# 256-byte allocation of the DMA tiles in a fused lightning-attention and mixture-of-depths kernel

## The chip, the cores and the metric

The kernel runs on one core of a Trainium2 chip. The metric is device time in microseconds (us) of one execution, the median of several runs. The core has the engines PE (TensorE; PEld is its weight load), DVE (VectorE), ACT (ScalarE) and POOL (GpSimd), SP (SyncE), which here only issues DMAs, and 16 DMA engines that move data between the chip's main memory (DRAM) and SBUF, the on-chip memory of 128 partitions.

## The reference

Four batches of eight heads with 768 positions of 64 elements, all float32. Attention runs in blocks of 64 positions with a decaying state, and its output is then taken as rows of 512 elements, of which the 128 best of each batch go through a two-layer expert:

```
for b in range(nb):                       # blocks of 64 positions, all batches and heads
    intra = (qb @ kb.T * Dmask) @ vb
    inter = (qb * lam_pow) @ kv_state
    out[:, :, sl] = intra + inter
    kv_state = lam_block * kv_state + (kb * rev_pow).T @ vb
x = out.transpose(0, 2, 1, 3).reshape(B, S, H * D)      # 4 x 768 x 512
scores = x @ w_gate
for b in range(B):
    top = the 128 rows of x[b] with the highest scores
    h = relu(x[b, top] @ w1); ye = h @ w2               # 512 x 1024 and 1024 x 512
    out[b, top] = x[b, top] + sigmoid(scores[b, top]) * ye
```

## The kernel before

The work is cut into 24 groups g, six per batch, of 128 positions of all eight heads. For every group `load` (L74) issues three DMAs on SP, `kn`, `qn` and `vn`, each 128 partitions by 8 heads by 64 elements: 256 KB in 1,024 pieces of 256 bytes, since one head's row of one position is 256 contiguous bytes in DRAM. The tiles lie in pool `ld` with six buffers per name, and a group's load is issued four to six groups ahead of its use (`loads_to`, `ahead`). On the same SP queue, in an order written out in the tables `WEIGHTS_WITH` and `STORES_WITH`, stand the 16 loads of the expert's weights (`w1_sb`, `w2_sb`, 128 rows of 2 KB each, L101 and L106) and the 24 stores of `x_b` (`store`, L380, 128 rows of 2 KB), so a store that waits for its data holds up the loads behind it.

In a group, PE transposes `kn` and `qn` (L207), forms the scores (L234 in the first nine, wide groups, L241 later), the state products from `kd` and `vn` (L274, L283), and the outputs (L326, L338, L346). POOL makes `kd`, the decayed keys (L191), the decayed queries `qs` (L219, L221) and the decayed state (L296). ACT copies the transposes and the output rows `x_b` (L368 to L376) out of PSUM. DVE masks the scores (L251, L257), adds the state (L315), makes the gate scores from `x_b` and `wg_b` (L388), and ranks rows (L418). In the wide groups PE transposes the gate scores (L408) right behind L388.

When a batch is ranked, POOL gathers its 128 rows from the output in DRAM (`fetch`, L483, tile `xs`), PE runs the expert (L496, L533, L545, the last batch in halves at L570), and DVE makes `y` or `y_half`, which POOL scatters back (L562, L586). Pieces of an earlier batch's expert are set between the steps of later groups by the table `PIECES`. Tiles are placed by the pools one behind the other, at multiples of 32 bytes.

Of the kernel before, what the change touches and what calls it, by code (L numbers as in the profile page):

```python
# [8 lines left out]
FP32 = mybir.dt.float32  # L9
# [8 lines left out]
def kernel(  # L18
# [14 lines left out]
    B, H, S, D = q.shape  # L33
    HD = H * D
    F = moe_w1.shape[1]
# [3 lines left out]
    NT = S // L  # L39
    NHP = H // 2  # L40
    NDC = HD // 128
    NFC = F // 128
# [3 lines left out]
    assert 0 <= CAP < S  # L46

    AHEAD = 6
    WIDE = 9
    WEIGHTS_WITH = {  # L50
        "kn": {11: 1, 12: 2, 13: 1, 14: 1, 15: 1, 16: 1},
# [11 lines left out]
    const = ctx.enter_context(tc.tile_pool(name="const", bufs=1))  # L63
    ld = ctx.enter_context(tc.tile_pool(name="ld", bufs=AHEAD))
    att = ctx.enter_context(tc.tile_pool(name="att", bufs=3))
    xpool = ctx.enter_context(tc.tile_pool(name="xpool", bufs=2))
    mod = ctx.enter_context(tc.tile_pool(name="mod", bufs=2))
# [6 lines left out]
    def load(g):  # L74
        b, c = divmod(g, NT)
        rows = slice(c * L, (c + 1) * L)
        tiles = []
        for name, src in (("kn", k), ("qn", q), ("vn", v)):
            t = ld.tile([128, H, D], FP32, name=name)
            nc.sync.dma_start(out=t[:], in_=src[b, :, rows, :].rearrange("h p d -> p h d"))  # L80
            tiles.append(t)
            for _ in range(WEIGHTS_WITH[name].get(g, 0)):
                weights.pop(0)()
            for s in STORES_WITH[name].get(g, ()):
                store(s)
        loaded[g] = tiles
# [4 lines left out]
    nc.scalar.dma_start(out=wg_row[:], in_=moe_w_gate.unsqueeze(0))  # L91
    for g in range(3):
        load(g)
    wg_b = const.tile([128, HD], FP32, name="wg_b")
    w1_sb = const.tile([128, NDC, F], FP32, name="w1_sb")
    w2_sb = const.tile([128, NFC, HD], FP32, name="w2_sb")

    def w1_load(f0, n, c):
        def do():
# [76 lines left out]
    x_bs, scs = {}, {}  # L176
# [6 lines left out]
    def wide(g):  # L183
        return g < WIDE

# [175 lines left out]
    def outputs(g):  # L361
        b, t = divmod(g, NT)
        if t == 0:
            x_bs[b] = xpool.tile([128, NT, NHP, 2, D], FP32, name="x_b")
            scs[b] = xpool.tile([128, NT], FP32, name="sc")
        x_b = x_bs[b]
        if wide(g):
            nc.scalar.copy(  # L368
                out=x_b[:, t].rearrange("p b a e -> p a b e"),
                in_=o_[:, :, : NHP * D].rearrange("p a (b e) -> p a b e", e=D),  # L370
            )
            return
        po = [o_[:, hh, : NHP * D].rearrange("p (b e) -> p b e", e=D) for hh in range(2)]
        nc.scalar.copy(out=x_b[:, t, :, 0, :], in_=po[0])
        for c in range(2):
            nc.scalar.copy(out=x_b[half[c], t, :, 1, :], in_=po[1][half[1 - c]])  # L376

    def store(g):
        b, t = divmod(g, NT)
        nc.sync.dma_start(  # L380
            out=out[b, t * L : (t + 1) * L, :],
            in_=x_bs[b][:, t].rearrange("p a b e -> p (a b e)"),
        )
# [9 lines left out]
    def rows_upto(b):  # L393
        return out[0 : b + 1].flatten_outer_dims()
# [83 lines left out]
    def rows_at(b, i):  # L478
        return bass.IndirectOffsetOnAxis(ap=toks[b, i][:, 0:1], axis=0)

    def fetch(b, i):
        xs = mod.tile([128, HD], FP32, name="xs")
        nc.gpsimd.indirect_dma_start(  # L483
            out=xs[:], out_offset=None, in_=rows_upto(b), in_offset=rows_at(b, i),
        )
        xss[b, i] = xs

    def expert(b, i, last=False):
# [51 lines left out]
        def back(f):  # L540
            def do():
                if f == 0:
                    keep["py"] = bank(hold=True)
                py = keep["py"]
                nc.tensor.matmul(  # L545
                    py[:], lhsT=keep["hs"][:, f, :], rhs=w2_sb[:, f, :],
                    start=(f == 0), stop=(f == NFC - 1),
                )
                if f + 1 == NFC:
                    after.append(finish)  # L550
            return do

        def finish():
            py = keep["py"]
            held.clear()
            free[:] = [x for x in free if x is not py] + [py]
            y = mod.tile([128, HD], FP32, name="y")
            nc.vector.scalar_tensor_tensor(
                out=y[:], in0=py[:], scalar=keep["g"][:], in1=xss[b, i][:],
                op0=ALU.mult, op1=ALU.add,  # L560
            )
            nc.gpsimd.indirect_dma_start(  # L562
                out=rows_upto(b), out_offset=rows_at(b, i), in_=y[:], in_offset=None,
            )

        def half_back(f, c):
            def do():
                if f == 0:
                    keep["py"] = bank()
                nc.tensor.matmul(  # L570
                    keep["py"][:, : HD // 2], lhsT=keep["hs"][:, f, :],
                    rhs=w2_sb[:, f, c * (HD // 2) : (c + 1) * (HD // 2)],
                    start=(f == 0), stop=(f == NFC - 1),
                )
                if f + 1 == NFC:
                    half_finish(c)
            return do

        def half_finish(c):
            cs = slice(c * (HD // 2), (c + 1) * (HD // 2))  # L580
            y = mod.tile([128, HD // 2], FP32, name="y_half")
            nc.vector.scalar_tensor_tensor(
                out=y[:], in0=keep["py"][:, : HD // 2], scalar=keep["g"][:],
                in1=xss[b, i][:, cs], op0=ALU.mult, op1=ALU.add,
            )
            nc.gpsimd.indirect_dma_start(  # L586
                out=rows_upto(b).rearrange("r (c e) -> (r c) e", c=2),
                out_offset=bass.IndirectOffsetOnAxis(ap=keep["at"][:, c : c + 1], axis=0),
                in_=y[:], in_offset=None,
            )  # L590
# [54 lines left out]
    def products(n):  # L645
        for _ in range(min(n, len(pieces))):
            pieces.pop(0)()

    def ahead(g):
        return min(4 + max(0, (g - 12) // 2), AHEAD)  # L650

# [4 lines left out]
    def loads_to(n):  # L656
        while next_load[0] < min(n, NG):
            load(next_load[0])
            next_load[0] += 1
# [12 lines left out]
    def get(b):  # L672
        for i in range(NGR):
            fetch(b, i)

    for g in range(-1, NG):
# [16 lines left out]
        if wide(g):  # L693
# [5 lines left out]
            if g >= 0:  # L699
                next_state(2 * g + 2)  # L700
                from_scores(g)
                outputs(g)
                if g not in kept:
                    store(g)
            else:
                state_products(0)
                next_state(0)
# [38 lines left out]
        now = PIECES.get(g, (1, 1, 1))  # L746
        if g == WIDE:
            products(1)
# [19 lines left out]
        products(now[1])  # L768
        from_scores(g)
        outputs(g)  # L770
        if g not in kept:
            store(g)
# [77 lines left out]
```

## Time and profile before

| what | value |
|---|---|
| median of 3 runs | 177.38 us (176.01 to 177.85) |
| the profiled execution | 176.31 us, of which the span from the first to the last instruction is 174.5 us |
| PE busy | 161.6 us (93%), granted clock at its upper level through the span |
| other engines busy | DVE 101.7, POOL 92.7, ACT 71.9 us |
| bytes moved by DMA | 31.96 MB in 81,475 packets |

Busy time of PE is modelled from pipelined matmuls, so a busy PE is not PE at its peak, and idle time of an engine off the path costs nothing. What counts for a change to DMA is which idle time a DMA ended. A packet is what a DMA engine moves as one unit: here 256 bytes for `kn`, `qn`, `vn`, 2 KB for weights and stores.

### The profile page before, as it was taken

The page shows a single profiled execution, that of the slowest core. Times are in us where ns is not written, and L with a number is a line of the kernel's source. Part 1 is how long each engine was busy: PE and PEld are TensorE (multiplying, and loading weights), DVE is VectorE, ACT ScalarE, POOL GpSimd, SP SyncE. Part 2 cuts the span into 40 slices and gives each one's busy share as a digit, 9 for nine tenths or more (in the row PEclk, how much of TensorE's full clock was granted, in tenths as well). Part 3 has the DMA queues.
Part 4 walks back from the last instruction along what each step waited for, and adds up shares of the span by engine and source line. Part 5 has one row for each costly group of instructions (what it writes and reads, how often), then busy time and mean ns, then how long its engine had stood idle before and what let it go on. Part 6 is the DMA issues. An engine that isn't in the chain of part 4 may idle for free.

```text
span 174.5 us, 7862 instructions
## 1 busy us (share of the span) xinstructions
PE 161.6 (93%) x3440; PEld 133.1 (76%) x3440; DVE 101.7 (58%) x227; ACT 71.9 (41%) x192; POOL 92.7 (53%) x101
## 2 busy tenths in 40 slices
PE   6898999999998999998999999999899899989990
PEld 6767888788786989765768999866669698459970
DVE  2566966777946834756547994675477856340011
ACT  2244365553344635543535544633555354013100
POOL 2249975818796554466595856455777700220022
PEclk9999999999999999999999999999999999999999
DMA  4999899999989999998999897998931111011000
GB/s 91 219 219 193 193 227 244 236 280 274 243 202 266 261 260 274 269 282 198 240 263 215 210 208 170 270 309 202 227 147 64 64 64 60 0 60 64 0 30 30
DMA packets 81475, 31.96 MB, mean 183 GB/s; under 512 B 75809, under 2 KB 75809, under 8 KB 81442
## 3 DMA queue, kind: packets, MB, share of 16 engines
q1 hardware_dynamic: 80640, 29.37, 71.0%
q0 software_dynamic: 656, 2.10, 4.0%
q8 instruction: 27, 0.44, 1.1%
q14 instruction: 6, 0.05, 0.1%
q10 hardware_dynamic: 146, 0.01, 0.0%
HBM read 24.12 MB, written 7.34 MB: 180 GB/s over the span
## 4 chain that ended last, share of the span: by engine, by line
PE 67%; DMA 12%; issue 6%; POOL 5%; DVE 4%; ACT 2%; SPq 2%; POOLq 1%; DVEq 0%
PE m L533 15%; PE m L207 9%; PE m L545 9%; DMA w_sb<-in_moe_w_dram 6%; PE o L338 5%; PE o L326 4%; PE o L346 4%; PE su L283 4%; DMA vn<-in_v_dram 3%; PE su L241 3%; PE m L274 3%; DVE xg L388 2%; PE m L137 2%; PE su L234 2%; PE m L570 2%
## 5 line engine op out<-in xcount | busy, mean ns | idle before, releaser
L418 DVE SCALAR_TENSOR_TENSOR table<-sc_row,sc,lead 128x128 bf16<-128x128 f32 (+5 forms) x24 | 28.1, 1170 | 14.6 <-ACT sc_row L411 14.0
L533 PE MATMUL m<-xsT,w_sb 128*128 128x128 f32 x256 | 34.1, 282 | 0.7 <-ACT xsT L503 0.5
L533 PEld LDWEIGHTS m<-xsT,w_sb 128*128 128x128 f32 x256 | 30.6, 192 | 1.7 <-ACT xsT L503 0.7
L221 POOL TENSOR_TENSOR qs<-qT,qpow 128x512 f32<-128x512 f32 x15 | 21.0, 1400 | 13.5 <-ACT qT L211 12.0
L388 DVE CUSTOM_DVE_ANT_0 xg<-x_b,wg_b 128x512 f32<-128x512 f32 x24 | 21.7, 903 | 8.7 <-ACT x_b L368 8.1
L545 PE MATMUL m<-w_sb,hs 128*128 128x512 f32 x48 | 24.9, 621 | 0.4 <-DMA w_sb<-in_moe_w_dram 0.4
L296 POOL TENSOR_TENSOR decayed<-state,decay 128x256 f32<-128x256 f32 x25 | 18.6, 745 | 12.4 <-DVE state L315 11.7
L537 ACT ACTIVATE hs<-m 128x128 f32<-128x128 f32 x32 | 8.9, 278 | 25.6 <-PE m L533 24.0
L315 DVE TENSOR_TENSOR state<-su,decayed 128x256 f32<-128x256 f32 x25 | 10.5, 421 | 14.3 <-PE su L283 9.2
L211 ACT COPY qT<-m 128x512 f32<-128x512 f32 x24 | 14.1, 586 | 9.8 <-PE m L207 6.7
L191 POOL TENSOR_TENSOR kd<-kn,kpow 128x512 f32<-128x512 f32 x15 | 16.2, 1082 | 0.5 <-DMA kn<-in_k_dram 0.5
L211 ACT COPY kT<-m 128x512 f32<-128x512 f32 x24 | 14.2, 592 | 3.6 <-PE m L207 3.6
L326 PE MATMUL o<-state,qs 64*64 64x64 f32 x672 | 15.3, 224 | 0.0
L207 PE MATMUL m<-ident,qn 128*128 128x128 f32 x96 | 15.1, 281 | 0.0
L207 PE MATMUL m<-ident,kn 128*128 128x128 f32 x96 | 14.9, 279 | 0.0
L411 ACT COPY sc_row<-m 128x128 f32<-128x128 f32 x24 | 6.3, 264 | 20.4 <-PE m L408 17.8
L326 PEld LDWEIGHTS o<-state,qs 64*64 64x64 f32 x672 | 12.4, 134 | 2.7 <-issue 2.3
L219 POOL TENSOR_TENSOR qs<-qT,qpow 128x512 f32<-128x512 f32 x7 | 9.8, 1404 | 6.9 <-ACT qT L211 6.9
L191 POOL TENSOR_TENSOR kd<-kn,kpow_w 128x512 f32<-128x512 f32 x9 | 9.9, 1100 | 6.0 <-DVE kpow_w L148 5.2
L207 PEld LDWEIGHTS m<-ident,qn 128*128 128x128 f32 x96 | 11.4, 144 | 2.0 <-issue 1.1
L283 PE MATMUL su<-vn,kd 64*64 64x64 f32 x432 | 10.4, 221 | 2.4 <-DMA vn<-in_v_dram 1.1
L346 PEld LDWEIGHTS o<-vn,p 64*64 64x64 f32 x480 | 8.4, 134 | 5.0 <-ACT sc_row L411 2.3
(85 smaller groups left out, 256.2 us busy)
## 6 DMA issues: line engine op xcount, KB each, us to landing
kn<-in_k_dram SPq DMA_DIRECT2D x24, 256.0 KB, 5.4
qn<-in_q_dram SPq DMA_DIRECT2D x24, 256.0 KB, 5.3
vn<-in_v_dram SPq DMA_DIRECT2D x24, 256.0 KB, 5.6
out_dram<-x_b SPq DMA_DIRECT2D x24, 256.0 KB, 4.6
w_sb<-in_moe_w_dram SPq DMA_DIRECT2D x16, 256.0 KB, 5.4
xs<-out_dram,tok POOLq DMA_INDIRECT x4, 4.5
out_dram<-y,tok POOLq DMA_INDIRECT x3, 3.4
out_dram<-y_half,half_at POOLq DMA_INDIRECT x2, 2.4
```

Source lines behind the costliest of these rows:

```text
L191: nc.gpsimd.tensor_tensor(out=kd[:], in0=loaded[g][0][:], in1=pw[:].rearrange("p a b -> p (a b)").unsqueeze(2).broadcast_to([128, H, D]), ...
L207: nc.tensor.transpose(tp[:, hp * L : (hp + 1) * L], in_=t[:, 2 * hp : 2 * hp + 2, :], identity=ident[:])
L211: nc.scalar.copy(out=dst[:].rearrange("p a i -> p (a i)"), in_=tp[:])
L221: nc.gpsimd.tensor_tensor(out=qs[:].rearrange("p a (c i) -> p a c i", c=2), in0=qTs[g].rearrange("p a (c i) -> p a c i", c=2), in1=qpow[:, ...
L283: nc.tensor.matmul(su[half[hh], c, NHP * C + hp * D : NHP * C + (hp + 1) * D], lhsT=kd[half[c], h, :], rhs=vn[half[c], h, :], start=True, ...
L296: nc.gpsimd.tensor_tensor(out=t[:], in0=states[n][:], in1=(decay_w if wide(g) else decay)[:], op=ALU.mult)
L326: nc.tensor.matmul(o_[half[c if wide(g) else hh ^ c], hh, hp * D : (hp + 1) * D], lhsT=qs[half[hh], hp, half[c]], rhs=states[n][half[hh], ...
L346: nc.tensor.matmul(o_[half[hh ^ c], hh, hp * D : (hp + 1) * D], lhsT=p[half[c], hh, hp * C : (hp + 1) * C], rhs=vn[half[c], 2 * hp + hh, : ...
L388: nc.vector.tensor_tensor_reduce(out=xg[:], in0=x_bs[b][:, t].rearrange("p a b e -> p (a b e)"), in1=wg_b[:], scale=1.0, scalar=0.0, op0=A ...
L418: nc.vector.scalar_tensor_tensor(out=table[:, : (t + 1) * L], in0=rows_[b][:, : (t + 1) * L], scalar=scs[b][:, t : t + 1], in1=lead[:, (NT ...
L533: nc.tensor.matmul(ph, lhsT=w1_sb[:, dc, f * 128 : (f + 1) * 128], rhs=keep["xsT"][:, dc, :], start=(dc == 0), stop=(dc == NDC - 1),)
L545: nc.tensor.matmul(py[:], lhsT=keep["hs"][:, f, :], rhs=w2_sb[:, f, :], start=(f == 0), stop=(f == NFC - 1),)
```

## The change

Tiles of ten names are allocated at a multiple of 256 bytes on each partition: nine that a DMA writes or reads, and the gate vector `wg_b`, which ACT writes. No instruction is added, removed or moved on any engine: the lists of the five engines are the same but for source line numbers, which rise by one behind the new constant.

```diff
+    LINE = 256
...
-            t = ld.tile([128, H, D], FP32, name=name)
+            t = ld.tile([128, H, D], FP32, name=name, align_bytes=LINE)
...
-    wg_b = const.tile([128, HD], FP32, name="wg_b")
-    w1_sb = const.tile([128, NDC, F], FP32, name="w1_sb")
-    w2_sb = const.tile([128, NFC, HD], FP32, name="w2_sb")
+    wg_b = const.tile([128, HD], FP32, name="wg_b", align_bytes=LINE)
+    w1_sb = const.tile([128, NDC, F], FP32, name="w1_sb", align_bytes=LINE)
+    w2_sb = const.tile([128, NFC, HD], FP32, name="w2_sb", align_bytes=LINE)
...
-            x_bs[b] = xpool.tile([128, NT, NHP, 2, D], FP32, name="x_b")
+            x_bs[b] = xpool.tile([128, NT, NHP, 2, D], FP32, name="x_b", align_bytes=LINE)
...
-        xs = mod.tile([128, HD], FP32, name="xs")
+        xs = mod.tile([128, HD], FP32, name="xs", align_bytes=LINE)
...
-            y = mod.tile([128, HD], FP32, name="y")
+            y = mod.tile([128, HD], FP32, name="y", align_bytes=LINE)
...
-            y = mod.tile([128, HD // 2], FP32, name="y_half")
+            y = mod.tile([128, HD // 2], FP32, name="y_half", align_bytes=LINE)
```

The built programs give every tile's byte address on its partition. All buffers of one name have the same distance past a multiple of 256:

| tile | first buffer before | past a multiple of 256 | first buffer after | past a multiple of 256 |
|---|---|---|---|---|
| `kn` | 74,976 | 224 | 75,776 | 0 |
| `qn` | 87,264 | 224 | 88,320 | 0 |
| `vn` | 99,552 | 224 | 100,864 | 0 |
| `wg_b` | 18,592 | 160 | 18,688 | 0 |
| `w1_sb` | 20,640 | 160 | 20,992 | 0 |
| `w2_sb` | 37,024 | 160 | 37,632 | 0 |
| `x_b` | 150,752 | 224 | 152,320 | 0 |
| `xs` | 191,904 | 160 | 193,536 | 0 |
| `y` | 208,416 | 32 | 210,432 | 0 |
| `y_half` | 212,576 | 96 | 214,784 | 0 |

The tiles behind them move along: `kd`, for one, from 224 to 32 past a multiple of 256. `lam_b`, whose rows are 32 bytes, stays at 128 past. The highest byte used grows from 214,624 to 216,832.

## Rows read from the trace of the kernel before

**Rows 1.** The page: engines' busy time, and the 40 slices of the span.

```profile
PE 161.6 (93%) x3440; PEld 133.1 (76%) x3440; DVE 101.7 (58%) x227; ACT 71.9 (41%) x192; POOL 92.7 (53%) x101
...
PE   6898999999998999998999999999899899989990
...
PEclk9999999999999999999999999999999999999999
DMA  4999899999989999998999897998931111011000
GB/s 91 219 219 193 193 227 244 236 280 274 243 202 266 261 260 274 269 282 198 240 263 215 210 208 170 270 309 202 227 147 64 64 64 60 0 60 64 0 30 30
```

**Rows 2.** PE's waits: who was waited for, us in total, times, longest.

```profile
PE m L408 <- DVE sc L388: 1.3, 4, 0.6
PE su L283 <- DMA vn<-in_v_dram: 1.1, 3, 0.5
...
PE su L283 <- POOL kd L191: 0.4, 1, 0.4
PE m L496 <- DMA xs<-out_dram,tok: 0.4, 1, 0.4
PE m L545 <- DMA w_sb<-in_moe_w_dram: 0.4, 1, 0.4
...
PE m L533 <- DMA w_sb<-in_moe_w_dram: 0.3, 1, 0.3
```

**Rows 3.** POOL's waits for the keys: us in total, times, longest.

```profile
POOL kd L191 <- DMA kn<-in_k_dram: 1.3, 3, 0.8
```

**Rows 4.** DMA view, 5 to 15 us: packets; then queue, packets, MB, share.

```profile
DMA packets 8628, 2.18 MB, mean 218 GB/s; under 512 B 8628, under 2 KB 8628, under 8 KB 8628
...
q1 hardware_dynamic: 8628, 2.18, 130.5%
```

**Rows 5.** SP's queue in order of time: start, us it took, what.

```profile
9.44 1.10 SPq L80 DMA_DIRECT2D vn<-in_v_dram  x1
...
63.78 0.38 SPq L80 DMA_DIRECT2D kn<-in_k_dram  x1
```

**Rows 6.** The DMA view, 121.8 to 122.8 us, the last loads.

```profile
DMA packets 1116, 0.29 MB, mean 285 GB/s; under 512 B 1114, under 2 KB 1114, under 8 KB 1116
...
q1 hardware_dynamic: 1116, 0.29, 125.5%
```

**Rows 7.** The DMA view, 90 to 105 us, loads alone on q1.

```profile
q1 hardware_dynamic: 10470, 2.64, 82.4%
```

**Rows 8.** SP's waits, the longest: who was waited for, us, times, longest.

```profile
SPq L380 <- ACT x_b L376: 11.4, 3, 6.0
...
SPq L80 <- POOL decayed L296: 4.0, 3, 3.0
SPq L80 <- POOL kd L191: 3.2, 5, 0.9
```

**Rows 9.** The DMA view, 2 to 5 us: lam_b, in rows of 32 bytes.

```profile
q10 hardware_dynamic: 127, 0.01, 2.2%
```

**Rows 10.** The DMA view, 130 to 150 us: stores of x_b.

```profile
q1 hardware_dynamic: 576, 1.05, 14.1%
```

**Rows 11.** The DMA view, 133.7 to 135 us: a scatter of y.

```profile
q0 software_dynamic: 79, 0.26, 54.1%
```

**Rows 12.** Single lines' instructions: duration ns min/median/max, first and last start us.

```profile
L388 DVE CUSTOM_DVE_ANT_0 xg<-x_b,wg_b x24: 678/842/1564, 14.4 to 145.5; 128x512 f32<-128x512 f32 x24
...
L515 DVE CUSTOM_DVE_ANT_0 xg<-xs,wg_b x4: 676/680/1746, 60.5 to 156.2; 128x512 f32<-128x512 f32 x4
...
L207 PE MATMUL m<-ident,qn x96: 272/273/421, 6.4 to 135.5; 128*128 128x128 f32 x96
...
L496 PE MATMUL m<-ident,xs x16: 272/273/327, 53.2 to 155.0; 128*128 128x128 f32 x16
```

**Rows 13.** The page: q1, packets, MB, share of 16 engines over the span.

```profile
q1 hardware_dynamic: 80640, 29.37, 71.0%
```

## The prediction

> **What bounds the kernel now.** First the page: PE is busy 161.6 of 174.5 us, at the upper clock level throughout, and the slices show it full from the first to the last but a few us, while the DMA row is also near full for the first 28 slices, some 122 us [rows 1]. Both are candidates, and the change touches only DMA, so the question is how much of PE's idle time a DMA ended. PE's list of waits answers it: three waits for `vn` cost 1.1 us, one each for `xs`, a `w_sb` of the first layer and one of the second 0.4, 0.4 and 0.3, together 2.2 us; one for `kd`, which stands behind a gather, 0.4 [rows 2]. So all that a faster stream of transfers can give directly is 2.2 to 2.6 us of 176. POOL's three waits for `kn` add 1.3 us of its own idle time [rows 3], of which PE feels a part at most in the start.
>
> Then I asked how near its limit the stream is. From 5 to 15 us, with loads alone queued, 8,628 packets take 130.5% of 16 engines [rows 4]: 1.305 x 160 / 8,628 = 24.2 ns each, overlapping, and one starts on each engine every 160 / 8,628 = 18.5 ns. That is a full stream at 218 GB/s: SP needs 1.10 us to issue one 256 KB load here, against 0.38 us for one where the queue has room [rows 5]. Later it is not full: the last loads run at 285 GB/s, 1.255 x 16 / 1,116 = 18.0 ns a packet and one start per engine every 14.3 ns [rows 6], and from 90 to 105 us q1 has packets for 82.4% of the time only [rows 7]. What holds SP there is its own order: stores wait 11.4 us for `x_b`, loads 4.0 and 3.2 us for buffers that POOL still reads [rows 8]. A faster engine does not shorten those.
>
> **The change part by part.** No instruction moves and no wait is added; ten names change their address.
>
> *Packets of the loads.* 24 groups x 3 loads x 1,024 = 73,728 packets of 256 bytes were written 224 past a multiple of 256, so each crosses one such boundary (32 bytes before it, 224 behind); after, none does. The trace has no load into an aligned tile, so the cost of the crossing is bounded. One end: nothing (a loss has no row: `lam_b` and all loads read DRAM as before, and crossing less is no more work). The other, for a packet that is not held up: the 127 packets on the queue of `lam_b`, nearly all 32 bytes at 128 past, cross nothing and take 0.022 x 48 us / 127 = 8.3 ns [rows 9]. A 2 KB store packet: 0.141 x 320 = 45.1 us, less some 0.5 us for 64 small completions, over 512 packets, 87.1 ns [rows 10]. From 256 bytes to 2 KB that is (87.1 - 18.0) / 1,792 = 0.0386 ns a byte, so a packet of 256 bytes that costs what the 32-byte one costs plus its 224 bytes more would take 8.3 + 8.6 = 16.9 ns: 1.1 ns under 18.0, or 6%. For a packet in the full stretch the far end is the spacing of the late loads, 14.3 instead of 18.5 ns, if the crossings are what fills the stretch; but the late loads cross the same boundary and run at 285 GB/s, so a crossing alone does not cost 18.5 ns. I take nothing, the value of the straight line through 256 bytes and 2 KB: it meets zero bytes at 18.0 - 256 x 0.0386 = 8.1 ns, close to the 7.1 that the 32-byte packet leaves when its own 32 bytes are taken off, so hardly anything is left for a crossing.
>
> *Stores, gathers and scatters.* `x_b` was read from 224 past, `y` from 32 past. The scatter of `y` has 64 packets of two rows (4 KB): 0.541 x 1.3 x 16 = 11.25 us, less 0.1 for 15 small ones, over 64 is 174 ns, or 87.0 per row of 2 KB, against 87.1 for a row of `x_b` [rows 10, 11]. Two very different offsets, one price: the offset costs nothing that these rows can show. If a row lost all that separates it from 2,048 x 0.0386 = 79 ns, 8 ns of 87 (9%), 24 stores of 128 rows would give 24 x 128 x 8 / 16 = 1.5 us of the stream, beside loads, on no path of PE but through the fetch behind a store. The last scatter, `y_half`, is the tail: 32 packets on 16 engines, two each, some 0.02 us at that price. I take nothing.
>
> The Trainium skill, "DMA: Bandwidth & Descriptors", section "How a descriptor splits into AXI transactions", speaks for the change: a transaction starts at a multiple of 256 bytes, and what lies between that and a descriptor's start is fetched for nothing, in beats of 32 bytes. By it a row of `x_b` would need 71 beats and one of `y` 65, 8% apart; the two rows above are equal, so this trace does not bear it out for reads of SBUF, and whether writes into SBUF follow it no run here shows. By its beats a load's packet would fall from 15 to 8; the rival below does without them.
>
> *Compute on the moved tiles.* DVE's gate product reads `x_b` at 224 past in 678 ns at least, the expert's reads `xs` at 160 past in 676; PE's transposes of `qn` at 224 and `xs` at 160 are both 273 ns [rows 12]. Engines do not feel the offset, so `kd` at 32 instead of 224 and the other moved tiles cost nothing.
>
> *Sum.* Against the profiled execution: 176.31 - 0 = 176.31 us, span 174.5 and 1.8 around it. If each load packet lost the 6%, the full stream would move 73,728 x 1.1 / 16 = 5.1 us less work, and a wait for a DMA with up to four transfers of 1.1 us before it would end 0.07 to 0.28 us sooner; over PE's six waits 0.4 to 1.7 us, below 2.2 in any case. The profiled run lies 1.07 us under the median of 177.38; the three runs and the profiled one have their middle at (176.31 + 177.38) / 2 = 176.85. For an unchanged kernel, between this and the median, I say **177.0**. About 1%, 1.8 us, is what a measurement of this kernel can tell from no change.
>
> **The rivals.**
>
> *A: the crossing is what fills the stream.* Then 24.2 ns fall to 18.0 or less in the first stretch, SP's 1.10 us per load to some 0.9, and the engines are ahead all through. For it: the full stretch at 18.5 ns a start has no other visible reason. Against it: crossing packets at 14.3 ns late. Its price is the list of waits: 2.2 us for the six on DMA, 0.4 for `kd`; what is late next is ACT and DVE in the wide groups (1.3 us on L388 stays [rows 2]) and SP's waits for `x_b`. 177.0 - 2.6 = 174.4; with half of the waits 175.7, with POOL's 1.3 us in full on top 173.1 [rows 3].
>
> *B: slower, by collisions of DVE and POOL.* Loads that land sooner let POOL start `kd` sooner, on top of L388, which needs 678 ns alone, 842 at the median and 1,564 at its longest [rows 12]. In the nine wide groups PE's transpose L408 follows L388 directly, and waited 1.3 us in four of them [rows 2]. Each group that goes from median to longest costs up to 0.72 us; from three on, 2.2 us, it decides: 179.2. Against it: POOL mostly waits for DVE's state or ACT's copies, not for `kn` (1.3 us, three times [rows 3]), so a sooner `kn` moves little. The Trainium skill, "SBUF — State Buffer", section "Who interferes with whom", says that a DVE instruction with two SBUF inputs contends with a GpSimd one that reads SBUF; the spread of L388 agrees.
>
> *C: the change does not take place*, because a slice of an aligned tile starts elsewhere. The addresses speak against it: buffers step by 2,048 bytes, weight slices by 2 KB, `x_b` groups by 2 KB, all multiples of 256. It would give the forecast's time in any case, and its chance is in the forecast's.
>
> **How the numbers follow.** Forecast (packets cost the same, or shrink by up to 6% that the waits do not repay): 0.63, 175.4 to 178.5. A: 0.28, 173.1 to 175.7, nearly all beyond 1%. B: 0.09, 179 and more. The range of 8 in 10 takes A from 174.0 on and leaves out B: 174.0 to 178.6; left out are some 0.10 of A and nearly all of B. Faster by over 1% (below 175.6) 0.28, within 1% 0.63, slower 0.09.
>
> **What the profile after would show.** For the forecast: 5 to 15 us still some 8,600 packets at 24 ns and 218 GB/s, late loads at 18.0 ns, SP's issues near 1.1 us in the first stretch, q1's share still near 71% of the span [rows 13], PE's six waits for DMA there in about the same sum. For A: the same window at 18 ns or less and over 250 GB/s, and no `vn` or `w_sb` in PE's waits. For B: L388's median above 1.2 us and PE's wait at L408 above 3 us. Wrong I would be most likely by the one thing no row shows: what a write into SBUF costs when it crosses no boundary of 256 bytes.

## The result, and the profile after

The changed kernel takes 173.85 us, the median of 22 runs (171.97 to 181.77), and the kernel before 177.56 (22 runs, 174.5 to 180.35): a ratio of 0.9867 with a 95% interval of 0.9826 to 0.9908. That is 2.4 us, or 1.3%, faster. The ratio compares only the runs of each kernel within 1.5% of its fastest, 15 of the 22 after and 8 of the 22 before, and so lies nearer 1 than the two medians, which are 3.7 us or 2.1% apart. Against the forecast of 177.0 us this is rival A. The time lies 0.15 us under the range as it stands; the ratio applied to the 177.38 of the runs first shown gives 175.0, inside it.

The profiled execution of the changed kernel took 173.58 us, span 171.8. First its page: busy time by engine, the slices of PE and DMA, and q1's share, the answers to [rows 1] and [rows 13].

```profile
PE 158.8 (92%) x3440; PEld 131.4 (77%) x3440; DVE 101.1 (59%) x227; ACT 71.7 (42%) x192; POOL 92.9 (54%) x101
...
PE   6898999999889899999997799999999999989990
...
DMA  4999999999999999999998999974411111011000
...
q1 hardware_dynamic: 80640, 29.37, 66.5%
```

The same packets and bytes hold 66.5% of 16 engines over the span, where they held 71.0%: 0.710 x 174.5 = 123.9 us of 16 engines against 0.665 x 171.8 = 114.2, so the packets take 9.7 us less on each engine. The DMA row falls off two slices earlier. Then the view that decides between the forecast and rival A, the DMA view from 5 to 15 us, the answer to [rows 4]:

```profile
DMA packets 9589, 2.43 MB, mean 243 GB/s; under 512 B 9588, under 2 KB 9588, under 8 KB 9588
...
q1 hardware_dynamic: 9588, 2.42, 107.0%
```

1.07 x 160 / 9,588 = 17.9 ns for a packet of 256 bytes instead of 24.2, and 243 GB/s instead of 218. SP's queue, the answer to [rows 5]:

```profile
6.12 0.85 SPq L81 DMA_DIRECT2D kn<-in_k_dram  x1
7.01 1.25 SPq L81 DMA_DIRECT2D qn<-in_q_dram  x1
8.31 0.82 SPq L81 DMA_DIRECT2D vn<-in_v_dram  x1
9.17 1.37 SPq L81 DMA_DIRECT2D kn<-in_k_dram  x1
```

Two of these issues take 0.82 to 0.85 us and two 1.25 to 1.37, where those of the same stretch before took 1.10 to 1.32. PE's waits, the whole answer but three rows of 0.7 us and less, beside [rows 2]:

```profile
PE m L409 <- DVE sc L389: 1.8, 5, 0.6
PE m L138 <- POOL zero L117: 1.5, 1, 1.5
PE su L284 <- issue: 1.2, 2, 0.9
PE m L497 <- DMA xs<-out_dram,tok: 1.2, 1, 1.2
...
PE o L347 <- issue: 0.5, 1, 0.5
PE su L242 <- issue: 0.5, 1, 0.5
```

The waits for `vn`, `w_sb` and `kd`, 2.2 us together before, are gone. So is the wait of 0.4 for the first batch's `xs` (at 53 us), but one of 1.2 for the second batch's has come (at 92 us), and two stalls of 0.5 us appear that end on no semaphore (L242, L347). Single lines, beside [rows 12] (duration ns min/median/max, first and last start us):

```profile
L389 DVE CUSTOM_DVE_ANT_0 xg<-x_b,wg_b x24: 679/844/1571, 13.3 to 142.8; 128x512 f32<-128x512 f32 x24
...
L208 PE MATMUL m<-ident,kn x96: 272/273/273, 5.2 to 133.7; 128*128 128x128 f32 x96
```

DVE's product on the moved tiles is as long as before. Not all of the 2.7 us between the two spans can be put down to the change. The transposes of `kn` take 272 or 273 ns from the first one on; in the profile of before the first transposes of `kn` and `qn` take 421 ns (for `qn` see [rows 12]). The trace's records of TensorE's granted clock begin, at the upper level (2.4 GHz), at 4.78 us here and at 7.23 us there, behind the same warm-up matmuls; for the time ahead of that there is no record, so the 9s of the PEclk row in [rows 1] say nothing of the first slice. Group 1's transposes of `qn` start, before and after, at

```profile
10.76 0.66 PE L207 MATMUL m<-ident,qn 128*128 128x128 f32 x4
```

```profile
9.62 0.66 PE L208 MATMUL m<-ident,qn 128*128 128x128 f32 x4
```

By then the changed kernel leads by 10.76 - 9.62 = 1.14 us, and it keeps that lead to group 9. The rest comes behind group 9. The moment of the rise differs from one profile to the next (4.6 to 7.5 us in twelve), and kernels in which it came late gained as much, below.

### The profile page after: what moved, and what is told of

It is laid out like the page before. It is cut to its first block, busy times and chain, and to the rows that moved or that the text cites. A ratio compares the mean times of both kernels' runs of the same rounds, so it can differ in the third digit from the quotient of the medians.

```text
span 171.8 us, 7862 instructions
## 1 busy us (share of the span) xinstructions
PE 158.8 (92%) x3440; PEld 131.4 (77%) x3440; DVE 101.1 (59%) x227; ACT 71.7 (42%) x192; POOL 92.9 (54%) x101
## 3 DMA queue, kind: packets, MB, share of 16 engines
q1 hardware_dynamic: 80640, 29.37, 66.5%
## 4 chain that ended last, share of the span: by engine, by line
PE 78%; DVE 6%; issue 5%; DMA 5%; ACT 3%; POOL 1%; POOLq 1%; DVEq 0%
PE m L534 18%; PE m L546 12%; PE m L208 11%; PE o L327 5%; PE o L347 5%; PE o L339 5%; PE su L242 4%; PE su L284 4%; DMA xs<-out_dram,tok 3%; PE m L275 3%; DVE xg L389 3%; PE m L409 2%; PE m L138 2%; PE m L571 2%; PE su L235 2%
## 5 line engine op out<-in xcount | busy, mean ns | idle before, releaser
L419 DVE SCALAR_TENSOR_TENSOR table<-sc_row,sc,lead 128x128 bf16<-128x128 f32 (+5 forms) x24 | 26.9, 1122 | 15.7 <-ACT sc_row L412 15.1
L534 PEld LDWEIGHTS m<-xsT,w_sb 128*128 128x128 f32 x256 | 30.5, 192 | 1.2 <-ACT xsT L504 0.7
L389 DVE CUSTOM_DVE_ANT_0 xg<-x_b,wg_b 128x512 f32<-128x512 f32 x24 | 22.2, 926 | 8.4 <-ACT x_b L369 7.8
L538 ACT ACTIVATE hs<-m 128x128 f32<-128x128 f32 x32 | 8.9, 277 | 24.6 <-PE m L534 24.6
L208 PE MATMUL m<-ident,qn 128*128 128x128 f32 x96 | 14.6, 275 | 0.0
L327 PEld LDWEIGHTS o<-state,qs 64*64 64x64 f32 x672 | 12.5, 134 | 2.5 <-issue 2.3
L208 PE MATMUL m<-ident,kn 128*128 128x128 f32 x96 | 14.4, 273 | 0.0
L347 PEld LDWEIGHTS o<-vn,p 64*64 64x64 f32 x480 | 8.5, 134 | 5.7 <-issue 2.8
L252 DVE TENSOR_TENSOR p<-su,mask_w 128x1024 f32<-128x1024 f32 x9 | 10.9, 1216 | 1.0 <-PE su L235 1.0
```

Of the source, the lines that this page charges most:

```text
L208: nc.tensor.transpose(tp[:, hp * L : (hp + 1) * L], in_=t[:, 2 * hp : 2 * hp + 2, :], identity=ident[:])
L252: nc.vector.tensor_tensor(out=p[:], in0=su[:], in1=mask_w[:].rearrange("p a b i -> p a (b i)"), op=ALU.mult,)
L327: nc.tensor.matmul(o_[half[c if wide(g) else hh ^ c], hh, hp * D : (hp + 1) * D], lhsT=qs[half[hh], hp, half[c]], rhs=states[n][half[hh], ...
L347: nc.tensor.matmul(o_[half[hh ^ c], hh, hp * D : (hp + 1) * D], lhsT=p[half[c], hh, hp * C : (hp + 1) * C], rhs=vn[half[c], 2 * hp + hh, : ...
L389: nc.vector.tensor_tensor_reduce(out=xg[:], in0=x_bs[b][:, t].rearrange("p a b e -> p (a b e)"), in1=wg_b[:], scale=1.0, scalar=0.0, op0=A ...
L419: nc.vector.scalar_tensor_tensor(out=table[:, : (t + 1) * L], in0=rows_[b][:, : (t + 1) * L], scalar=scs[b][:, t : t + 1], in1=lead[:, (NT ...
```

## The experiments

All kernels but the two with DMAs alone keep the changed kernel's order of instructions and its waits on every engine; all but null, after2 and rows2k differ in addresses alone. They set each tile at a chosen distance past a multiple of 256 (the first line is that of loads0):

```diff
+    PAST = {'kn': 0, 'qn': 0, 'vn': 0, 'wg_b': 160, ..., 'y_half': 96}
+    def placed(pool, n, name):
+        t = pool.tile([128, n + LINE // 4], FP32, name=name, align_bytes=LINE)
+        return t[:, PAST[name] // 4 : PAST[name] // 4 + n]
...
-            t = ld.tile([128, H, D], FP32, name=name, align_bytes=LINE)
+            t = placed(ld, HD, name).rearrange("p (h d) -> p h d", d=D)
```

Times and ratios, with what the two views that matter say of each kernel's profile. GB/s and ns a packet are those of the DMA view from 5 to 15 us, worked out as above; PE's waits are the sum of its waits for `qn`, `vn`, `kd`, `w_sb` and `xs`, in us. In the profiles of null and all64b the granted clock was at its lower level for a stretch (88.1 to 91.5 us and 9.9 to 13.3 us), so their waits, 3.4 and 3.0 us, are left out of the table. The rows come from four comparisons: the change; rest0, all128 and loads0; allb, all64 and rows2k; null, all64b, after2 and loads0b. Those of one comparison share their runs of the kernel before.

| kernel | loads' distance | ratio to before, 95% interval | GB/s | ns | PE's waits |
|---|---|---|---|---|---|
| before | 224 | 1 | 218 | 24.2 | 2.6 |
| null (before again) | 224 | 1.0033 (0.9971 to 1.0095) | 219 | 24.6 | |
| allb | 224 | 0.9958 (0.9905 to 1.0011) | 219 | 24.7 | 2.7 |
| rest0 | 224 | 1.0154 (1.0068 to 1.0240) | 218 | 24.6 | 4.4 |
| all128 | 128 | 0.9979 (0.9921 to 1.0037) | 220 | 24.2 | 0 |
| all64 | 64 | 0.9885 (0.9799 to 0.9970) | 220 | 24.8 | 3.1 |
| all64b (all64 again) | 64 | 0.9997 (0.9925 to 1.0070) | 220 | 25.1 | |
| the change | 0 | 0.9867 (0.9826 to 0.9908) | 243 | 17.9 | 1.2 |
| after2 (the change again) | 0 | 0.9885 (0.9830 to 0.9940) | 250 | 17.8 | 0.9 |
| loads0 | 0 | 0.9930 (0.9869 to 0.9991) | 253 | 17.8 | 0.6 |
| loads0b (loads0 again) | 0 | 0.9891 (0.9827 to 0.9956) | 246 | 17.8 | 0 |

**m_offsets: the DMAs alone.** Nothing is computed. Six loads of 1,024 pieces of 256 bytes for each of nine distances, then 2 KB rows in, then 2 KB rows out; between two stages DVE touches every tile:

```diff
+PASTS = (0, 16, 32, 64, 96, 128, 160, 192, 224)
...
+        for i in range(N):
+            src = (k, q, v)[i % 3]
+            nc.sync.dma_start(
+                out=at(i, past).rearrange("p (h d) -> p h d", d=64),
+                in_=src[(g + i // 3) % 4, :, rows, :].rearrange("h p d -> p h d"),
+            )
...
+    for s, past in enumerate(PASTS):
+        pieces(past, s)
```

> DMAs alone, no attention and no expert: six 256 KB loads in 256-byte pieces, back to back, for each of nine distances past a multiple of 256 bytes in SBUF (0, 16, 32, 64, 96, 128, 160, 192, 224), then six loads in 2 KB rows for 0, 32, 128, 160, 224, then stores in 2 KB rows for the same five. What it computes is not the reference. Theory 1 (a piece that crosses a multiple of 256 is two writes): only distance 0 gives packets of 18 ns and a stream over 250 GB/s; all others, 64, 128 and 192 too, give about 24 ns and 218 GB/s as before. Rival (it is a granule of 64 bytes that a write must fill): 0, 64, 128 and 192 are alike at 18 ns, and 16, 32, 96, 160, 224 at 24 ns. Rival (the stall is not made by the distance): all nine alike. Rows of 2 KB: a crossing costs one write in nine, so under 5% between distances.

The DMA view of three stages: 0 past (2.5 to 7.5 us), 64 past (30.5 to 37 us) and 224 past (79 to 86 us).

```profile
q1 hardware_dynamic: 5537, 1.40, 123.6%
```

```profile
q1 hardware_dynamic: 5754, 1.45, 131.3%
```

```profile
q1 hardware_dynamic: 5978, 1.51, 119.0%
```

That is 17.9 ns and 279 GB/s aligned, 23.7 ns and 223 GB/s at 64 past, 22.3 ns and 215 GB/s at 224 past. The other six distances lie at 22.6 to 23.5 ns and 203 to 221 GB/s by the same view. So it does not matter how far past: a tile at 64 or 128 is as slow as one at 16. A piece of 256 bytes that starts off a multiple of 256 always crosses one, so these stages cannot tell the start from the crossing; the text calls both the crossing. Rows of 2 KB into SBUF gave 261 to 338 GB/s over their stages, more than the 5% expected, but with no order in the distance (0 past: 286, 32: 261, 128: 318, 160: 338, 224: 280). Inside their stages, stores of 2 KB rows ran at 406 GB/s from an aligned tile and 381 to 383 from the four others.

**m_repeat: the same, with the same rows of DRAM in every stage and an aligned stage behind each crossing one.** It excludes that the 256-byte stages of m_offsets differed by the rows they read.

```diff
-PASTS = (0, 16, 32, 64, 96, 128, 160, 192, 224)
+PASTS = (224, 0, 128, 0, 32, 0)
...
-        pieces(past, s)
+        pieces(past, 0)
```

> DMAs alone again, now with the same source rows in every stage and the aligned stage between the others: six loads in 256-byte pieces each at 224, 0, 128, 0, 32, 0 past a multiple of 256, then six loads in 2 KB rows at 224, 0, 160, 0, 128, 0, then six stores in 2 KB rows at 224, 0, 224, 0. Not the reference's output. Theory 1 (a piece that crosses is two writes): each stage at 0 is at 18 ns a packet and over 270 GB/s inside, each other one at 22 to 24 ns and 213 to 226, whatever its place in the order. Rival (the first stage of a program is fast): the stages at 0 in second, fourth and sixth place are like the others. For 2 KB rows: the three stages at 0 within 5% of each other and of the rest; if the first micro-kernel's 267 to 345 GB/s came from the distance, they differ by more. Stores: 0 faster than 224 by about 4%.

Inside their bursts the DMA view gives the 256-byte stages 218, 272, 218, 273, 219 and 270 GB/s: slow, fast, slow, fast, slow, fast. Stores at 224, 0, 224, 0 past gave 382, 409, 381 and 405 GB/s. Loads of 2 KB rows again followed no distance: 267, 289 and 279 GB/s in the three aligned stages, so not within the expected 5% of each other, and 257 to 327 in the others. Read more finely, a crossing stage shows what the prediction lacked. Its DMA view for 128 past, first from 21 to 22 us, then from 22.8 to 26.5 us:

```profile
DMA packets 1111, 0.28 MB, mean 280 GB/s; under 512 B 1111, under 2 KB 1111, under 8 KB 1111
...
q1 hardware_dynamic: 1111, 0.28, 124.0%
```

```profile
DMA packets 3192, 0.81 MB, mean 218 GB/s; under 512 B 3192, under 2 KB 3192, under 8 KB 3192
...
q1 hardware_dynamic: 3192, 0.81, 133.8%
```

And the aligned stage ahead of it, from 13 to 15 us, well into its burst:

```profile
DMA packets 2204, 0.56 MB, mean 278 GB/s; under 512 B 2204, under 2 KB 2204, under 8 KB 2204
...
q1 hardware_dynamic: 2204, 0.56, 122.9%
```

At the front of a burst a crossing packet takes 1.24 x 16 / 1,111 = 17.9 ns and the stream runs at 280 GB/s, as if aligned. Behind that it takes 1.338 x 59.2 / 3,192 = 24.8 ns and the stream is held at 218. The aligned stage stays at 1.229 x 32 / 2,204 = 17.8 ns and 278 GB/s.

**loads0 and loads0b: only `kn`, `qn` and `vn` aligned.** The other seven tiles stand at their old distances (the diff above).

> Only kn, qn and vn at a multiple of 256; weights at 160, x_b 224, xs 160, y 32, y_half 96 past one, as before. Theory (the loads' pieces are what counts): all of the gain, ratio to the kernel before 0.982 to 0.992, packets of 256 bytes at 18 ns, stores still at 86 to 87 ns. Rival (the rest carries it): ratio 0.995 to 1.005.

> Only the tiles of k, q and v at multiples of 256, the other seven at the distances of before, again. The crossing theory: 0.984 to 0.994, most of the change's gain, with 245 to 255 GB/s in the window from 5 to 15 us. Rival, the gain needs all tiles: 0.995 to 1.003.

0.9930 and 0.9891: most of the gain or all of it is in the loads, and the intervals cover the change's own ratio. The first lies just outside the range that was expected, 0.982 to 0.992. In both profiles the clock rose late (7.1 and 7.5 us), so the gain does not need the early rise of the changed kernel's profile. PE's waits for DMA are 0.6 us in the one and none in the other. The 0.6 is put down to `vn` at L554, whose matmuls read `w_sb` and `hs`; the last section says what it likely is.

**rest0: everything aligned but the loads.** Against loads0:

```diff
-    PAST = {'kn': 0, 'qn': 0, 'vn': 0, 'wg_b': 160, ..., 'y_half': 96}
+    PAST = {'kn': 224, 'qn': 224, 'vn': 224, 'wg_b': 0, ..., 'y_half': 0}
```

> Everything at a multiple of 256 but kn, qn and vn, which stay 224 past one. Theory: no gain, ratio 0.995 to 1.005, 24 ns packets from 5 to 15 us as before; late stores at 84 instead of 87 ns, which no wait on the path feels. Rival: 0.982 to 0.992.

No gain: 1.0154. Its window from 5 to 15 us is that of before (218 GB/s), and PE's waits for the loads are back:

```profile
PE su L290 <- DMA vn<-in_v_dram: 1.3, 3, 0.5
PE su L290 <- POOL kd L198: 1.2, 1, 1.2
PE m L505 <- DMA xs<-out_dram,tok: 1.2, 1, 1.2
...
PE m L554 <- DMA w_sb<-in_moe_w_dram: 0.7, 1, 0.7
```

That it is slower than before by more than its interval, and not within the expected 0.995 to 1.005, no run explains. The medians of all its runs and of the kernel before beside it, 177.78 and 176.76 us, lie 0.6% apart. With six runs, and all64 moving by 1.1% between two comparisons, it stays open whether the loss is real.

**all128, all64, all64b, allb: all ten tiles at one distance, or at the old ones in the new layout.** Against loads0:

```diff
-    PAST = {'kn': 0, 'qn': 0, 'vn': 0, 'wg_b': 160, ..., 'y_half': 96}
+    PAST = {'kn': 128, 'qn': 128, 'vn': 128, 'wg_b': 128, ..., 'y_half': 128}
```

That is all128. all64 and all64b have 64 for every name; allb has the distances of the kernel before.

> All ten names 128 bytes past a multiple of 256, so at multiples of 64 and 128, yet every piece of 256 bytes crosses. Theory 1 (crossing): as before, ratio 0.995 to 1.005, packets at 24 ns in the first stretch. Rival (a 64-byte granule): as the changed kernel, 0.982 to 0.992, packets at 18 ns.

> The layout of loads0, rest0 and all128 (every tile in a slot 256 bytes larger, kd at 32) with the distances of the kernel before: 224, 160, 32, 96. Theory 1: as the kernel before, ratio 0.993 to 1.007. Rival (the layout itself, not the distances, carries part of the gain, as all128's 174.5 us would say): ratio 0.985 to 0.993. If the padded layout costs, as rest0's 177.8 us would say: 1.007 to 1.015.

> All ten names 64 bytes past a multiple of 256: every piece of a load crosses, 192 bytes before the boundary and 64 behind. Theory 1: packets near 24 ns from 5 to 15 us, ratio 0.993 to 1.007. Rival (a multiple of 64 is enough, and all128's middle of 174.5 us was no chance): 0.982 to 0.992.

> All ten tiles 64 bytes past a multiple of 256, again. The crossing theory: the loads run as before (216 to 222 GB/s in the window from 5 to 15 us) and so the time is 0.994 to 1.006 of before; the 0.9885 of the first time was scatter. Rival, something besides the loads' packets is won by placing all tiles at one distance (the same remainder for all, whichever it is): 0.983 to 0.992 again, with the window still at 216 to 222 GB/s.

allb holds the room that padding takes and the moved neighbours against the old distances: 0.9958, an interval that holds 1. all64 came out at 0.9885 although its loads run at 220 GB/s. This spoke against the crossing as the only cause, and was the reason to run it again: 0.9997 with the same 220 GB/s. all128, 0.9979, has a profile without a single wait of PE for DMA, though its loads cross; one profile of a crossing kernel may happen to miss them all. By the medians of all runs it even lies 1.3% under the kernel before (174.48 against 176.76 us), and it was not run again: whether its distance wins something besides the loads' packets is less well excluded than for all64.

**null and after2: the two kernels again, as a control of the comparison.** Their text is unchanged but for a comment.

```diff
+# the kernel before, unchanged
```

> The kernel before under another label, with one line of comment more: a control. If the interval of a comparison covers what moves the time (late waits, fetches of instructions, the clock's rise), the ratio is 0.994 to 1.006 and its interval holds 1. Rival: two programs of the same text differ by 1% or more here, from one loading to the next; then the ratio is off 1 by 0.01, its interval leaves out 1, and no ratio of the placed kernels within 0.985 to 1.015 says anything on distances. The window from 5 to 15 us moves 216 to 222 GB/s by both.

> The changed kernel again. The crossing theory: ratio 0.982 to 0.992 as in the first comparison (0.987), and 240 to 255 GB/s in the window from 5 to 15 us. Rival, scatter of the comparison: the ratio lands anywhere in 0.98 to 1.005.

null 1.0033, its interval holds 1; after2 0.9885. The six ratios of kernels with crossing loads have a mean of 1.0001, the four with aligned loads 0.9893, and of the ten only the first all64 lies on the other group's side. By the medians of all runs the two means are 0.998 and 0.984, about as far apart, with all128 on the other side (0.987). Against the same runs of the kernel before, loads0 lies 1.4% under the mean of rest0 and all128, and after2 and loads0b 1.3% under that of null and all64b. The profiles agree in the mean, though they scatter: PE waits 2.6 us for DMA in the mean of five crossing profiles (2.6, 2.7, 4.4, 0, 3.1) and 0.7 in that of four aligned ones, 1.9 us less, or 1.1%. all64's 3.1 comes from an execution of 178.36 us, 2% above that kernel's median.

**rows2k: still fewer packets.** k, q and v are loaded as whole rows of 2 KB instead of pieces of 256 bytes. The tiles then hold other elements, so another result is computed by the same instructions; it asks what a faster stream would be worth yet.

```diff
-            nc.sync.dma_start(out=t[:], in_=src[b, :, rows, :].rearrange("h p d -> p h d"))
+            whole = src[b].rearrange("h (r j) d -> (h r) (j d)", j=H)
+            nc.sync.dma_start(out=t[:].rearrange("p h d -> p (h d)"), in_=whole[rows, :])
```

> The changed kernel, with k, q and v loaded as contiguous rows of 2 KB instead of 1,024 pieces of 256 bytes; heads and positions are then mixed, so the output is not the reference's, but every instruction and wait is the same. A load's packets then cost the 16 engines 128 x 84 / 16 = 0.67 us instead of 1,024 x 14.4 / 16 = 0.92. It shows how much of the time is left to the stream once the crossings are gone. Theory (the waits for DMA that the change removed were nearly all there was): ratio to the kernel before 0.980 to 0.990, within 0.5% of the changed kernel. Rival (the stream still holds the middle of the kernel up): 0.960 to 0.978.

The stream from 5 to 15 us runs at 405 GB/s and q1 falls to 47.8% of the span, yet the kernel takes 1.0111 of before (1.0055 to 1.0167), outside both ranges that were named. Its waits of PE:

```profile
PE su L243 <- issue: 1.6, 1, 1.6
...
PE m L547 <- DMA qn<-in_q_dram: 1.1, 1, 1.1
PE su L236 <- issue: 1.0, 1, 1.0
PE o L348 <- issue: 0.7, 2, 0.4
```

The list has no wait for a load: L547 reads `w_sb` and `hs`, not `qn`, and its 1.1 us is likely a stall of the kind that the last section describes. Stalls without a semaphore, 3.3 us on the three other lines, stand in their place. Feeding PE faster than the aligned loads do has bought nothing here.

## Why the prediction went as it did

**The forecast and the range.** The forecast was no change, and the kernel became 1.3% faster by the mechanism of rival A, which had a chance of 0.28. That 175.0 still lies in the range of 174.0 to 178.6 is due to its lower end, which took in most of rival A, and not to the working of the forecast.

**What bounds the kernel, and the price of a faster stream: right in size.** PE's own list of waits gave 2.2 us for six waits on DMA and 0.4 for `kd`, 2.6 in all. Measured: 0.0133 x 177.56 = 2.4 us. Rival A's time of 174.4, within 173.1 to 175.7, was made from those rows, and the signs it named (18 ns or less, some 0.9 us for an issue, no `vn` or `w_sb` in PE's waits) are in the profile after, that of the issue in half of the rows shown; its "over 250 GB/s" stands at 243. That 2.6 and 2.4 agree so closely is partly luck: the same sum runs from 0 to 4.4 us in the profiles of kernels with crossing loads. Two readings were off. The two waits for `w_sb` are named the wrong way round (0.3 at L533, the first layer, and 0.4 at L545, the second [rows 2]), and the one at L545 was likely no wait for `w_sb` (last section). And the 82.4% of [rows 7] is no share of the time: packets overlap, and a full stretch reaches 130%.

**The packets of the loads: the step that failed.** "I take nothing" chose the near end of a bound whose far end, 14.3 ns between starts instead of 18.5, was right in kind: 160 / 9,588 = 16.7 ns now, 160 / 8,628 = 18.5 before, and 32 / 2,204 = 14.5 in m_repeat's aligned stage. The stream was given 9.7 us back, where the prediction's other bound, 6% of a packet, gave 5.1. The ground for it, and for the chance of 0.63, was that late loads cross the same boundary and take 18.0 ns at 285 GB/s [rows 6]. That row is one microsecond, and it is the front of a burst. The DMA view of the kernel before half a microsecond wide, directly behind it (123 to 123.5 us), had the other price:

```profile
DMA packets 355, 0.10 MB, mean 208 GB/s; under 512 B 354, under 2 KB 354, under 8 KB 354
...
q1 hardware_dynamic: 354, 0.09, 100.8%
```

1.008 x 8 / 354 = 22.8 ns. A packet of instructions (16 KB) falls into that half microsecond too; the start of the kernel shows the same turn without one. Before, from 3.4 to 4.2 us, and then from 5 to 7 us:

```profile
DMA packets 898, 0.23 MB, mean 286 GB/s; under 512 B 897, under 2 KB 897, under 8 KB 898
...
q1 hardware_dynamic: 896, 0.23, 125.2%
```

```profile
DMA packets 1750, 0.44 MB, mean 221 GB/s; under 512 B 1750, under 2 KB 1750, under 8 KB 1750
...
q1 hardware_dynamic: 1750, 0.44, 128.5%
```

17.9 ns and 286 GB/s, then 23.5 ns and 221 GB/s, all in the same kernel, into the same tiles. So a crossing costs nothing while a burst is young and some 6 ns a packet once it lasts. A price per packet, taken from a row of either kind, was the wrong model; a ceiling on the lasting rate, 218 GB/s against 278 in the stages of m_repeat shown above, is the one that fits. The rows for it were in the trace of before. What builds up in the first one or two microseconds, the runs do not show: that two neighbouring pieces share a 256-byte stretch which is then written twice was not tried apart from the crossing itself.

**The straight line through 32 bytes, 256 bytes and 2 KB** met the same trap: the 18.0 ns it went through was the price at the front of a burst, so that it left nothing for the crossing says nothing about a full stream.

**Stores and scatters: no gain, and that was right for the time.** The step from "two offsets, one price" to "the offset costs nothing" was not: 224 and 32 past are both past. Aligned, a row costs less: from 130 to 150 us the changed kernel has

```profile
q1 hardware_dynamic: 432, 0.79, 10.2%
```

for three stores, or (0.102 x 320 - 0.4) / 384 = 84 ns a row where [rows 10] gave 87.1; m_repeat's 409 and 405 against 382 and 381 GB/s say the same. In the same window rest0, with only the loads crossing, has (0.136 x 320 - 0.5) / 512 = 84 ns too and no gain, and loads0, with its stores at the old distance, (0.106 x 320 - 0.4) / 384 = 87 ns. Over 24 stores that is 24 x 128 x 3 / 16 = 0.6 us of the stream, which the ratios of loads0 and the change cannot tell. The Trainium skill, "DMA: Bandwidth & Descriptors", section "How a descriptor splits into AXI transactions", has transactions start at multiples of 256 bytes, and the runs bear out its direction, for writes into SBUF as well. An estimate from its beats (71 and 65) makes a row read from 224 past dearer by 9% than one from 32 past; inside their stages m_offsets has 383 and 382 GB/s for them, so the size does not follow.

**Compute on the moved tiles, and rival B: right.** L388's median went from 842 to 844 ns, PE's transposes stayed at 273. PE's wait at L408 rose from 1.3 to 1.8 us, far from the 3 us that would have shown rival B. **Rival C** is out by the windows.

**What is late next.** Rival A named L388 and SP's waits for `x_b`. Both came (1.8 us, and SP's 11.4 us for `x_b` became 17.0), but more was given back at a gather's `xs` (1.2 us where another had taken 0.4) and at stalls without a semaphore, about which the prediction says nothing. In this pair of profiles PE's idle time did not fall at all: 174.5 - 161.6 = 12.9 us before and 171.8 - 158.8 = 13.0 after, so new waits and stalls took the place of the old. The spans differ by PE's busy time, whose ends are modelled: 1.2 us of it lies ahead of group 1's `qn`, with the clock, and what the other 1.6 us is, no view here tells. In the mean of the profiles in the table PE is idle for 14.0 us in the five crossing kernels and 12.5 in the four aligned ones. So that the gain comes by way of PE's waits is borne out by the means, and not by the pair of profiles.

## What to carry to other kernels

Before a duration from a row is taken as the price of an access pattern, look at how long the stream has been full there: the first microsecond or two of a burst can show the price without its limit, so read a window in the middle of a long burst. Loads in pieces of 256 bytes into tiles at a multiple of 256 sustain about a quarter more here when nothing else is queued, and 64 or 128 past is no better than any other distance; what that was worth here was about the sum of the waits for DMA on the bounding engine, and not the 9.7 us that the stream was given back. When a wait is put down to a DMA, see whether the waiting line reads that tile, and whether other profiles name the same DMA at the same place. Where the effect is 1%, run the unchanged kernel as a control and every surprising ratio twice.

## What the runs showed that was not expected

**Stalls of PE with no semaphore.** In several profiles PE stops for 0.5 to 1.6 us in the middle of one line's matmuls, with nothing to wait for. The changed kernel's timeline has one (start, us it took, what):

```profile
49.63 0.56 PE L242 MATMUL su<-qT,kT 64*64 64x64 f32 x21
50.67 0.45 PE L242 MATMUL su<-qT,kT 64*64 64x64 f32 x11 [0.48 <-issue]
```

and rows2k the longest:

```profile
52.30 0.56 PE L243 MATMUL su<-qT,kT 64*64 64x64 f32 x21
54.44 0.34 PE L243 MATMUL su<-qT,kT 64*64 64x64 f32 x8 [1.57 <-issue]
```

Both stop after the same 21 matmuls. The same place of PE's program stalls in loads0 and loads0b too, and in all64, whose loads cross; in after2 and the six other profiles it does not. On the queue of instructions 27 packets of 16 KB pass in every profile (0.44 MB), one of which ends 1.2 us ahead of the second row in rows2k and 1.5 us ahead of that in the changed kernel. In the twelve profiles PE never passes this place sooner than 1.2 us after that packet ended: the five with the stall go on 1.2 to 1.5 us after it, the seven without pass 1.5 to 2.4 us after it.

A second place shows how such a stall can be taken for a wait. The 1,868th of PE's 3,440 matmuls, in the expert's second layer, is held up for 0.4 to 2.0 us in nine of the twelve profiles, with aligned loads and with crossing ones. The views put it down to `w_sb` in before (L545 in [rows 2]), rest0 and all64, to `qn` in rows2k, to nothing in null, allb, all64b and after2, and to `vn` in loads0. In null and in loads0 it reads

```profile
PE m L546 <- issue: 2.0, 1, 2.0
```

```profile
PE m L554 <- DMA vn<-in_v_dram: 0.6, 1, 0.6
```

In all twelve the matmul starts 1.3 to 1.6 us after the end of a 16 KB packet of the instruction queue. Without this place PE's waits in the table are 2.2 us in the mean of the five crossing profiles and 0.5 in the four aligned ones.

So I take these stalls for fetches of PE's instructions that come late. This is argued from the profiles; no run held the fetch back or made it early. Nor is it shown that aligned loads make them worse: counted by the `issue` rows of PE's waits and with the second place, they sum to 2.3 us in the mean of the five crossing profiles and 2.6 in the four aligned ones, but to 5.4 in rows2k, which may be why rows2k is no faster.

**The start of the upper clock level wanders.** The same warm-up matmuls were followed by the upper level at 4.6 to 7.5 us in twelve profiles. Both profiles of the changed kernel are early (4.8 and 4.6); whether a kernel's text has a part in it, two profiles don't tell. In the one pair shown it is 1.1 of 2.7 us.
